# A load moved behind masks, a cast moved to GpSimd and weight sums moved up in a fused attention and feed-forward kernel

## The chip, the cores and the metric

The kernel runs on one core of a Trainium2 chip. The metric is the device time of one execution in microseconds (us). Before the change the median of three runs is 211.47 us (211.43 to 211.76).

The core has TensorE (PE; its weight loads are shown as PEld), VectorE (DVE), ScalarE (ACT) and GpSimd (POOL), which compute, and SyncE (SP), which here only issues transfers. Each works through its own queue in order. A transfer (DMA) is issued by SP, ACT or POOL and then carried out by 16 DMA engines that all queues share.

## What is computed

Linear attention with decay over 4 batches, 8 heads, 768 positions of 64 values, and then a feed-forward layer of width 2048 on the 512 joined head outputs:

```python
    for b in range(nb):
        qb, kb, vb = (q[:, :, sl], k[:, :, sl], v[:, :, sl])
        intra = np.einsum('bhic,bhjc->bhij', qb, kb) * Dmask[None]
        intra = np.einsum('bhij,bhjd->bhid', intra, vb)
        inter = np.einsum('bhid,bhde->bhie', qb * lam_pow[None], kv_state)
        out[:, :, sl] = intra + inter
        kb_dec = kb * rev_pow[None]
        kv_state = lam_block[None, :, None, None] * kv_state + np.einsum('bhsd,bhse->bhde', kb_dec, vb)
...
    xn = (x - mu) / np.sqrt(var + 1e-06) * g_ln
    ch = np.maximum(xn @ w_ch1, 0.0) @ w_ch2
    return (x + ch).astype(np.float32)
```

## The kernel before

**Units.** The work is cut into 12 units. A unit is 256 positions of one batch with all 8 heads, two tiles of 128 rows. Units 0 to 3 are the first 256 positions of the four batches (no state comes in), 4 to 7 the next, 8 to 11 the last. In the change's name, pairs of tiles are counted from one: the second pair is unit 1, the fourth is unit 3.

**What a unit goes through.**
1. Its k, q and v (512 KB each in float32) are loaded into a pool with three buffers for each of the three (`load_in`, `load_window`, `fill`). SP issues them at line 76, from unit 6 on in two halves at line 80.
2. k is cast to bfloat16 (`in_k_one`, line 231; `in_k`, line 215), q is multiplied with the decays (`in_q_one`, line 236; `in_q`, line 226), v likewise (`in_v`, line 242, into `vb`).
3. k and q are transposed: units 0 to 2 by TensorE (`transpose_pe`, line 250), the later ones by a DMA transpose that SP issues (`transpose_dma`, line 257), into `kqT`.
4. TensorE makes the scores of two halves (`scores`, line 273, into two PSUM buffers `sc`), VectorE masks them into bfloat16 (`mask`, line 283). Unit 0's second half is masked in two steps: ScalarE copies it (line 290), VectorE multiplies (line 294).
5. TensorE makes the new states (`kv`, line 307). In unit 3 VectorE decays the first of them (line 313), adds the second (`state_sum`, line 317), and GpSimd decays that one (line 313).
6. `av` (line 419) and `inter` (line 432) sum the output in PSUM. `inter` is called twice; between the calls VectorE makes a small copy of the output, `seen` (`reader`, line 443), for which the second call waits.
7. The rows are copied and centred (`norm`, lines 458 to 470), transposed (`to_xT`, lines 486 and 493) and go into the feed-forward part.

**Feed-forward.** `mlp(g)` gives two kinds of steps for unit g: `m1`, a product with part of W1 (line 530, at the start line 641) with a relu by ScalarE (line 533 or 644), and `m2`, a product with W2. For units 0 to 3, `m2` is plain (line 667); VectorE evicts a finished tile (line 691). From unit 4 on it is a scheme with seven products for eight (line 565) that needs sums of blocks of W2, called `wt`. VectorE makes these once, in `w_sums(c, n)` for four chunks c of W2: n = 0 is two subtractions or additions (lines 787 and 788), n = 1 two more (790 and 791), each 128x512 float16 with both inputs in SBUF. Their first use is in unit 4's part, at 100 us.

**Weights.** W1 and W2 come in four chunks each, cast on the way by GpSimd's transfer queue (`load_w1`, line 117; `load_w2`, line 120). `load_w1(0)` is issued between the steps of unit 0, chunks 1 to 3 between GpSimd's work for unit 1, in this order: q, first half; chunk 1; q, second half; chunk 2; v of unit 1; chunk 3. GpSimd then waits for chunk 2 to land (`behind`, line 728) before it clears one column of unit 2's k buffer (`open_in` with a gate, line 91). SP's load of that k waits for this column, so that it can't start earlier. Unit 3's load is held back by a gate of the same kind.

**The order** is written out by hand: a long list of calls at the end of the kernel, in which `units(n)` takes the next n steps of the feed-forward list `plan`. Each call puts its instructions at the end of the queues of the engines that it names. The PSUM tag `mm` has four buffers that go round among m1, m2, `kv` and others.

At the start, `load_window(1)` issues k, q and v of unit 1 on SP directly behind those of unit 0. Around unit 3, the order is: states of unit 2 (`s0(2)`), the casts of unit 3's k on VectorE and the rest of its inputs on GpSimd, its two transposes, v of unit 4, two steps, `s3(2)` with the first `inter` and the copy `seen`, two steps, `s4(2)` with the second `inter`. After it, the steps number 8 to 12 stand around the transposes of unit 2's rows; then GpSimd's inputs of unit 4 and this:

```python
    units(5)
    w_sums(0, 0)
    w_sums(0, 1)
    units(2)
    w_sums(1, 0)
    units(1)
    s1(3)
```

The five steps are the four of unit 1's second tile in `m2`, whose last one is evicted by VectorE, and the first `m1` step of unit 2; the three others are `m1` steps of unit 2.

Of the kernel before, what the change touches and what calls it, by code (L numbers as in the profile page):

```python
# [17 lines left out]
def kernel(  # L18
# [11 lines left out]
    nc = tc.nc  # L30
# [35 lines left out]
    qkv_in = {}  # L66
# [5 lines left out]
    def fill(got, name, u, hs, eng=None):  # L72
        eng = eng or nc.sync
        src = dict(k=k, q=q, v=v)[name]
        if u < LB:
            eng.dma_start(got[:, hs], source(src, u, hs))  # L76
            return
        cc, b = divmod(u, B)
        for j in range(2):
            eng.dma_start(got[:, hs, j * D:(j + 1) * D],  # L80
                          src[b, hs, cc * W + j * C:cc * W + (j + 1) * C, :].rearrange("h p d -> p h d"))
# [6 lines left out]
    def open_in(u, gate):  # L88
        qkv_in[u] = {name: inp.tile([128, H, 2 * D], F32, tag=name + "in", name=name + "in") for name in "kqv"}
        if gate:  # L90
            nc.gpsimd.memset(qkv_in[u]["k"][:, 0, 0:1], 0.0)

    def load_in(u, name, eng):
        got = qkv_in[u][name]
        fill(got, name, u, slice(0, H), eng)
        qkv_in[u][name] = got.rearrange("p h (j d) -> p h j d", j=2)

    def load_window(u, after_pool=False, parts=1):
        got = {name: inp.tile([128, H, 2 * D], F32, tag=name + "in", name=name + "in") for name in "kqv"}
        if after_pool:  # L100

            nc.gpsimd.memset(got["k"][:, 0, 0:1], 0.0)
        n = H // parts
        order = [(name, i) for i in range(parts) for name in "kq"] + [("v", i) for i in range(parts)]
        for name, i in order:
            hs = slice(i * n, (i + 1) * n)
            fill(got[name], name, u, hs)
        qkv_in[u] = {name: f.rearrange("p h (j d) -> p h j d", j=2) for name, f in got.items()}
# [89 lines left out]
    def open_window(u):  # L198
        kq = wk.tile([128, 2, NP, 2, 2, D], BF16, tag="kq", bufs=3, name="kq")
        vb = wk.tile([128, H, 2, D], BF16, tag="vb", bufs=4, name="vb")  # L200
        st[u] = dict(kq=kq, vb=vb)
        if u < XB:
            st[u]["kqT"] = wk.tile([128, 2, NP, 2, 128], BF16, tag="kqT", bufs=3, name="kqT")

    def part(a, dst, hs):

        return dst[:, a, hs.start // 2:hs.stop // 2].rearrange("p a j e d -> p a e j d")
# [3 lines left out]
    def in_k(u, eng, hs=ALL):  # L211
        src = qkv_in[u]["k"][:, hs].rearrange("p (a e) j d -> p a e j d", e=2)
        dst = part(0, st[u]["kq"], hs)
        for j in range(2):
            (eng.copy if eng is nc.scalar else eng.tensor_copy)(dst[:, :, :, j], src[:, :, :, j])
# [13 lines left out]
    def in_k_one(u, eng, j):  # L229
        src = qkv_in[u]["k"].rearrange("p (a e) j d -> p a e j d", e=2)  # L230
        (eng.copy if eng is nc.scalar else eng.tensor_copy)(part(0, st[u]["kq"], ALL)[:, :, :, j], src[:, :, :, j])

    def in_q_one(u, eng, j):
        src = qkv_in[u]["q"].rearrange("p (a e) j d -> p a e j d", e=2)
        lq = (lam_q[:, :, j] if u < LB else lam_p[:, 0, :]).rearrange("p (a e) -> p a e", e=2)
        eng.tensor_tensor(part(1, st[u]["kq"], ALL)[:, :, :, j], src[:, :, :, j],  # L236
                          lq[:, :, :, None].to_broadcast([128, NP, 2, D]), op=ALU.mult)

    def in_v(u, eng, hs=ALL):
        n = hs.stop - hs.start  # L240
        lv = lam_v[:, hs, :, None] if u < LB else lam_p[:, 1, hs, None, None]
        eng.tensor_tensor(st[u]["vb"][:, hs], qkv_in[u]["v"][:, hs], lv.to_broadcast([128, n, 2, D]), op=ALU.mult)  # L242
# [17 lines left out]
    def scores(u, hf, early=False):  # L260

        s = st[u]
        kT, qT = s["kqT"][:, 0], s["kqT"][:, 1]
        if early:
            sc = [mm_tile([128, 2, 2, 128], F32, f"sce{e}") for e in range(2)]
        else:
            sc = [ps.tile([128, 2, 2, 128], F32, tag="sc", bufs=2, name=f"sc{e}") for e in range(2)]
        mA = wk.tile([128, 2, 2, 2, 128], BF16, tag=f"mA{hf}", name=f"mA{hf}")
        for i in range(2):
            for jk in range(2):  # L270
                for ab in range(2):
                    for e in range(2):
                        nc.tensor.matmul(sc[e][half[ab], i, jk, :], lhsT=kT[half[e], 2 * hf + i, jk, half[ab]],  # L273
                                         rhs=qT[half[e], 2 * hf + i, :, half[ab]],
                                         start=(i == 0 and jk == 0), stop=(i == 1 and jk == 1), skip_group_check=True)
        s[f"mA{hf}"] = mA
        s[f"sc{hf}"] = sc
# [8 lines left out]
    def mask_by_act(u, hf):  # L286

        s = st[u]
        for e in range(2):
            nc.scalar.copy(s[f"mA{hf}"][:, e], s[f"sc{hf}"][e])  # L290
        kp = keep_h.rearrange("p a b t -> p a (b t)")
        for e in range(2):
            m = s[f"mA{hf}"][:, e]
            nc.vector.tensor_tensor(m, m, kp[:, None, :, :].to_broadcast([128, 2, 2, 128]), op=ALU.mult)

    def kv(u, tag="mm"):

        s = st[u]
        cc, b = divmod(u, B)
        n_ab = 2 if (cc + 1) * W < S else 1  # L300
        bufs = dict(mm=4, sc=2, po=1)[tag]
        pk = [ps.tile([128, 2, NP, D], F32, tag=f"po{ab}" if tag == "po" else tag, bufs=bufs, name=f"pk{ab}")[:, 0] for ab in range(n_ab)]
        for p in range(NP):
            for j in range(2):
                for e in range(2):
                    for ab in range(n_ab):
                        nc.tensor.matmul(pk[ab][half[e], p, :], lhsT=s["kq"][half[ab], 0, p, j, e],
                                         rhs=s["vb"][half[ab], 2 * p + e, j],
                                         start=(p == 0 and j == 0), stop=(p == NP - 1 and j == 1), skip_group_check=True)
        s["pk"] = pk  # L310
# [9 lines left out]
    def new_state(u, ab, eng):  # L320

        s = st[u]
        b = u % B
        if ab == 1 and len(s["pk"]) == 1:
            return
        old = state.get(b)
        if ab == 0:
            s["S"] = [(old, old)]
        Sn = wk.tile([128, NP, D], BF16, tag="S", bufs=12, name="Sn")
        if old is None and eng is nc.scalar:  # L330
            for p in range(NP):
                nc.scalar.activation(Sn[:, p], s["pk"][ab][:, p], ACT.Identity, scale=lam_s[:, p:p + 1])
        elif old is None:
            decay(nc.vector, Sn, s["pk"][ab])
        else:
            tmp = s.pop("tmp", None) or state_sum(u, ab)
            decay(eng, Sn, tmp)
        state[b] = Sn
        if ab == 0:
            s["S"].append((Sn, Sn))  # L340
# [394 lines left out]
            nc.tensor.matmul(t, lhsT=ident, rhs=rhs, start=True, stop=True)  # L735

    open_window(0)
    load_window(1)
    in_k(0, nc.vector, HA)
    transpose_pe(0, 0, (0, 1))  # L740
    keep_busy(1, "po0")
# [22 lines left out]
    mask(0, 0)  # L764
    scores(0, 1, early=True)
    mask_by_act(0, 1)
    kv(0)
    new_state(0, 0, nc.scalar)
    av(0, (0, 1))
# [11 lines left out]
    def w_sums(c, n):  # L781
        v = w2[c].rearrange("p (k e) d -> p k e d", e=2)
        w = DM // 2
        b11, b12, b21, b22 = v[:, :, 0, 0:w], v[:, :, 0, w:], v[:, :, 1, 0:w], v[:, :, 1, w:]
        t1, t2, t3, t4 = (wt[c][:, :, i] for i in range(4))
        if n == 0:
            nc.vector.tensor_tensor(t1, b12, b11, op=ALU.subtract)  # L787
            nc.vector.tensor_tensor(t3, b12, b22, op=ALU.add)
        else:
            nc.vector.tensor_tensor(t2, b11, t3, op=ALU.subtract)  # L790
            nc.vector.tensor_tensor(t4, t2, b21, op=ALU.add)
# [28 lines left out]
    def s1(u):  # L820
        kv(u)
        scores(u, 0)
        new_state(u, 0, nc.gpsimd)
        mask(u, 0, (0,))
        new_state(u, 1, nc.gpsimd)
        mask(u, 0, (1,))
# [195 lines left out]
    def units(n):  # L1022
        for _ in range(n):
            f, *a = next(steps)
            f(*a)
# [15 lines left out]
    units(2)  # L1041
    s0(2)
    open_window(3)
    in_k_one(3, nc.vector, 0)
    in_k_one(3, nc.vector, 1)
    in_q_one(3, nc.gpsimd, 0)
    in_q_one(3, nc.gpsimd, 1)
    in_v(3, nc.gpsimd)
# [21 lines left out]
    in_q_one(4, nc.gpsimd, 0)  # L1070
    in_q_one(4, nc.gpsimd, 1)
    in_v(4, nc.gpsimd)
    units(5)
    w_sums(0, 0)
    w_sums(0, 1)
    units(2)
    w_sums(1, 0)
    units(1)
    s1(3)
    store(0)  # L1080
    transpose_dma(4, 0)
# [273 lines left out]
```

## Time and profile before

| what | value |
|---|---|
| median of three runs | 211.47 us |
| the profiled execution | 212.06 us |
| its span | 210.4 us |
| mean granted TensorE clock | 0.997 |
| moved over the span | 36.39 MB, 173 GB/s |
| PE busy from 15 to 20 us | 3.55 of 5.00 us |
| PE busy from 45 to 50 us | 3.96 of 5.00 us |
| PE busy from 60 to 65 us | 4.45 of 5.00 us |
| PE busy from 80 to 100 us | 20.00 of 20.00 us |

The span is the time from the first to the last thing that the profiler records; the device time has another 1.7 us around it. A line of the timeline gives start, duration, engine, line of the code, operation, what is written and read, how many instructions are taken together, and in brackets the idle time before it with what ended it. A line of the waits gives the engine and line that waited, for whom, the total in us, how often, and the longest. The chain in order of time follows back from the last instruction what released each step; SPq is SP's queue of transfers. In the view of the DMAs q1 is SP's queue and q0 is GpSimd's, each with packets, megabytes and the share of the 16 engines.

### The profile page before, as it was taken

What the parts mean: (1) busy time and instruction counts of PE and PEld (TensorE: products, weight loads), DVE (VectorE), ACT (ScalarE), POOL (GpSimd) and SP (SyncE); (2) the same over time, 40 slices, a digit from 0 to 9 for tenths busy, and PEclk for the clock granted to TensorE, in tenths of its full rate; (3) what the DMA queues carried; (4) which work ended last, traced back from release to release, by engine and by line L of the source; (5) the groups of instructions that cost most, each with busy time, mean ns of one, the idle gap of its engine ahead of it and who ended that gap; (6) DMA issues with size and microseconds to landing.
All of it is one profiled execution on the core that took longest, in us unless ns stands there. A gap on an engine that the chain in (4) does not pass through costs nothing.

```text
span 210.4 us, 7229 instructions
## 1 busy us (share of the span) xinstructions
PE 197.7 (94%) x3099; PEld 157.1 (75%) x3099; DVE 132.8 (63%) x274; ACT 121.6 (58%) x280; POOL 83.8 (40%) x116
## 2 busy tenths in 40 slices
PE   2987999989989999999999999999999999999991
PEld 0476889535666577568888898888888888888881
DVE  2683660534585966659698785667877857865252
ACT  3864679617155368528656675585596575652620
POOL 4657049218469150527246350862274202002020
PEclk9999999999999999999999999999999999999998
DMA  4999999999999998995896999897989020078403
GB/s 113 300 253 190 185 272 198 194 287 247 219 301 222 218 182 151 191 247 93 174 230 101 184 200 155 195 219 114 214 155 199 7 50 3 21 143 280 113 12 89
DMA packets 91042, 36.39 MB, mean 173 GB/s; under 512 B 65153, under 2 KB 88193, under 8 KB 91010
## 3 DMA queue, kind: packets, MB, share of 16 engines
q1 hardware_dynamic: 86400, 31.53, 72.8%
q0 software_dynamic: 4224, 4.19, 12.7%
q8 instruction: 24, 0.39, 0.8%
q10 hardware_dynamic: 386, 0.20, 0.4%
q14 instruction: 8, 0.07, 0.1%
HBM read 27.27 MB, written 6.29 MB: 160 GB/s over the span
## 4 chain that ended last, share of the span: by engine, by line
PE 69%; DMA 15%; DVE 5%; POOL 4%; SPq 3%; issue 1%; POOLq 0%; ACT 0%; DVEq 0%
PE pm L530 31%; PE pm L667 11%; DMA qin<-in_q_dram 7%; PE pwd L565 6%; PE pwa L565 6%; PE pwc L565 6%; DMA kin<-in_k_dram 5%; DMA w<-in_moe_w_ch_dram 3%; PE pwb L565 3%; SPq L76 3%; PE po L432 1%; DVE wt L787 1%; POOL kq L226 1%; DVE x L578 1%; PE po L406 1%
## 5 line engine op out<-in xcount | busy, mean ns | idle before, releaser
L530 PE MATMUL pm<-xT,w 128*128 128x256 bf16 x736 | 84.7, 273 | 0.0
L530 PEld LDWEIGHTS <-w 128*128 128x128 bf16 x736 | 70.5, 98 | 9.5 <-DVE Smid L388 0.3
L533 ACT ACTIVATE hT<-pm 128x512 f16<-128x512 f32 x92 | 53.9, 599 | 30.1 <-PE pm L530 30.0
L667 PE MATMUL pm<-w,hT 128*128 128x512 f16 x128 | 30.2, 380 | 0.0
L565 PEld LDWEIGHTS <-hs 128*128 128x128 f16 x256 | 24.9, 98 | 2.9
L590 POOL TENSOR_TENSOR x<-ev_u,x 128x256 f32<-128x256 f32 x8 | 5.9, 738 | 49.7 <-ACT ev_u L589 38.3
L313 POOL TENSOR_TENSOR Sn<-Stmp,lam_s 128x256 bf16<-128x256 f32 x16 | 9.8, 616 | 38.0 <-DVE Stmp L317 19.8
L548 DVE TENSOR_TENSOR hs<-hT 128x1024 f16<-128x1024 f16 x16 | 12.8, 800 | 15.6 <-ACT hT L533 15.6
L283 DVE TENSOR_TENSOR mA<-sc,keep 128x512 bf16<-128x512 f32 x20 | 13.1, 684 | 13.4 <-PE sc L273 13.4
L667 PEld LDWEIGHTS <-hT 128*128 128x128 f16 x128 | 11.7, 98 | 12.1
L565 PEld LDWEIGHTS <-hT 128*128 128x128 f16 x192 | 18.8, 98 | 2.2
L458 ACT ACTIVATE x<-po 128x512 f32<-128x512 f32 x18 | 10.6, 590 | 9.2 <-PE po L432 5.7
L460 DVE SCALAR_TENSOR_TENSOR xc<-po,nmean,g_row 128x512 bf16<-128x512 f32 x18 | 12.9, 745 | 3.6 <-ACT nmean L459 3.5
L242 POOL TENSOR_TENSOR vb<-vin,lam_v 128x1024 bf16<-128x1024 f32 (+1 forms) x7 | 11.8, 1691 | 4.2 <-DMA vin<-in_v_dram 4.2
L503 ACT ACTIVATE sq<-x,nmean 128x512 bf16<-128x512 f32 x18 | 12.9, 719 | 0.3
L242 POOL TENSOR_TENSOR vb<-vin,lam_p 128x1024 bf16<-128x1024 f32 x6 | 11.4, 1896 | 2.9 <-DMA vin<-in_v_dram 2.9
L236 POOL TENSOR_TENSOR kq<-qin,lam_q 128x512 bf16<-128x512 f32 x8 | 8.2, 1046 | 5.4 <-DMA qin<-in_q_dram 5.4
L494 ACT COPY xT<-xt 128x512 bf16<-128x512 bf16 x10 | 5.8, 585 | 7.7 <-PE xt L493 7.7
L236 POOL TENSOR_TENSOR kq<-qin,lam_p 128x512 bf16<-128x512 f32 x9 | 9.3, 1042 | 2.5 <-DMA qin<-in_q_dram 2.5
L578 DVE SCALAR_TENSOR_TENSOR x<-pwd,rstd,x 128x256 f32<-128x256 f32 x16 | 7.7, 482 | 3.5 <-POOL x L598 3.5
L578 DVE SCALAR_TENSOR_TENSOR x<-pwa,rstd,x 128x512 f32<-128x512 f32 (+1 forms) x16 | 9.1, 613 | 0.8
L565 PE MATMUL pwa<-w,hT 128*128 128x256 f16 x64 | 9.6, 273 | 0.0
(129 smaller groups left out, 301.1 us busy)
## 6 DMA issues: line engine op xcount, KB each, us to landing
out_dram<-x SPq DMA_DIRECT2D x22, 256.0 KB, 3.8
w<-in_moe_w_ch_dram POOLq DMA_DIRECT2D x8, 512.0 KB, 7.8
kin<-in_k_dram SPq DMA_DIRECT2D x14, 256.0 KB, 4.9
qin<-in_q_dram SPq DMA_DIRECT2D x14, 256.0 KB, 5.0
vin<-in_v_dram SPq DMA_DIRECT2D x14, 256.0 KB, 5.2
kin<-in_k_dram SPq DMA_DIRECT2D x5, 512.0 KB, 6.2
qin<-in_q_dram SPq DMA_DIRECT2D x5, 512.0 KB, 7.0
vin<-in_v_dram SPq DMA_DIRECT2D x5, 512.0 KB, 7.6
```

Source lines behind the costliest of these rows:

```text
L236: eng.tensor_tensor(part(1, st[u]["kq"], ALL)[:, :, :, j], src[:, :, :, j], lq[:, :, :, None].to_broadcast([128, NP, 2, D]), op=ALU.mult)
L242: eng.tensor_tensor(st[u]["vb"][:, hs], qkv_in[u]["v"][:, hs], lv.to_broadcast([128, n, 2, D]), op=ALU.mult)
L283: nc.vector.tensor_tensor(s[f"mA{hf}"][:, e], s[f"sc{hf}"][e], kp[:, None, :, :].to_broadcast([128, 2, 2, 128]), op=ALU.mult)
L458: nc.scalar.activation(x, po, ACT.Copy, accum_out=sm)
L460: nc.vector.scalar_tensor_tensor(xc, in0=po, scalar=nm, in1=g_row, op0=ALU.add, op1=ALU.mult)
L503: nc.scalar.activation(sq, s["x"][:, ab], ACT.Square, bias=s["nmean"][:, ab:ab + 1], accum_out=ss[:, ab:ab + 1])
L530: nc.tensor.matmul(pm[:, b, :], lhsT=w1[n // W2K][:, kk, (n % W2K) * 128:(n % W2K + 1) * 128], rhs=xT_of[g][:, kk, 0:N], start=(b == 0 and ...
L533: nc.scalar.activation(hT[:, u * NB:(u + 1) * NB, 0:N], pm, ACT.Relu)
L548: nc.vector.tensor_tensor(s13, b[:, :, 1:2, :].to_broadcast([128, n, 2, 128]), b[:, :, 0:4:3, :], op=ALU.subtract)
L565: nc.tensor.matmul(pr[bank], lhsT=lhs(r), rhs=rhs, start=(first and r == 0), stop=(r == KB // 2 - 1), skip_group_check=True)
L578: nc.vector.scalar_tensor_tensor(out, in0=in0, scalar=r[ab], in1=in1, op0=ALU.mult, op1=ALU.add)
L667: nc.tensor.matmul(acc[i], lhsT=hT[:, kk, i * 128:(i + 1) * 128], rhs=w2[kk // W2K][:, kk % W2K, :], start=(kk == 0), stop=(kk == KB - 1))
```

## The change

Three parts.

1. `load_window(1)` becomes `open_in(1, False)` with loads of k and q only. The load of v stands behind `mask_by_act(0, 1)`: VectorE clears one column of v's buffer after the two masking products of line 294, and SP's load of v waits for this.
2. The two casts of unit 3's k move from VectorE's queue to GpSimd's, in front of the q products of that unit.
3. The three `w_sums` calls move two steps up. In VectorE's queue, the four sums of chunk 0 now stand in front of the eviction of unit 1's second tile instead of behind it; the two of chunk 1 stand directly behind that eviction. On the other engines no order changes by this.

```diff
     open_window(0)
-    load_window(1)
+    open_in(1, False)
+    load_in(1, "k", nc.sync)
+    load_in(1, "q", nc.sync)
     in_k(0, nc.vector, HA)
...
     mask_by_act(0, 1)
+    nc.vector.memset(qkv_in[1]["v"][:, 0, 0:1], 0.0)
+    load_in(1, "v", nc.sync)
     kv(0)
...
     open_window(3)
-    in_k_one(3, nc.vector, 0)
-    in_k_one(3, nc.vector, 1)
+    in_k_one(3, nc.gpsimd, 0)
+    in_k_one(3, nc.gpsimd, 1)
     in_q_one(3, nc.gpsimd, 0)
...
-    units(5)
+    units(3)
     w_sums(0, 0)
     w_sums(0, 1)
     units(2)
     w_sums(1, 0)
-    units(1)
+    units(3)
     s1(3)
```

## The prediction, before the changed kernel was run

> **What bounds the kernel now.** I read the page's busy shares and slices first, then the waits of PE, then the chain in order of time, then the timeline around each PE gap. TensorE is busy 94% of the span, and from 80 us on it is never idle for more than 0.1 us in a stretch of 20: what is to be won lies before 65 us.
>
> ```profile
> PE 197.7 (94%) x3099; PEld 157.1 (75%) x3099; DVE 132.8 (63%) x274; ACT 121.6 (58%) x280; POOL 83.8 (40%) x116
> ...
> PE   2987999989989999999999999999999999999991
> ...
> DMA  4999999999999998995896999897989020078403
> ```
>
> The slices show PE falling to 7 or 8 only in the first 65 us, and the DMA engines full up to 80 us. The waits of PE over the whole span name the gaps:
>
> ```profile
> PE pm1t L641 <- DMA w<-in_moe_w_ch_dram: 1.5, 1, 1.5
> PE po L432 <- DVE seen L443: 1.0, 1, 1.0
> PE sc L273 <- DVE mA L283: 0.6, 1, 0.6
> ```
>
> Each is one wait: 1.45 us until W1's first chunk has landed (PE could go at 16.07, goes at 17.53), 1.04 us and 0.55 us until VectorE has done something. The chain in order of time shows who sets the second:
>
> ```profile
> 34.95 11.44 DMA kin<-in_k_dram
> 46.39 0.02 issue
> 46.41 0.76 DVE kq L231 x2
> 47.17 0.09 DVE seen L443
> 47.26 0.04 issue
> 47.30 0.31 PE po L432 x8
> ```
>
> k of unit 3 takes 11.44 us to land; its casts stand in VectorE's queue ahead of the small copy `seen` for which PE waits. The timeline of VectorE from 55 to 65 us shows the third:
>
> ```profile
> 57.88 0.43 DVE L791 TENSOR_TENSOR wt<-wt,w 128x512 f16<-128x512 f16 x1
> 58.23 2.12 DVE L787 TENSOR_TENSOR wt<-w 128x512 f16<-128x512 f16 x1
> 60.28 0.41 DVE L788 TENSOR_TENSOR wt<-w 128x512 f16<-128x512 f16 x1
> 60.61 0.41 DVE L313 TENSOR_TENSOR Sn<-pk,lam_s 128x256 bf16<-128x256 f32 x1
> 60.95 0.68 DVE L283 TENSOR_TENSOR mA<-sc,keep 128x512 bf16<-128x512 f32 x1
> ```
>
> One sum over W2 takes 2.12 us where its neighbours take 0.42, and unit 3's state and masks stand behind it. PE's third gap (62.05 to 62.60) is the wait for the second mask, which ends at 62.55.
>
> **What the Trainium skill says.** "SBUF — State Buffer", section "Who interferes with whom": a VectorE tensor_tensor with two inputs in SBUF and a GpSimd instruction that reads SBUF exclude each other for a whole instruction, and the one that issues second blocks; an instruction with one SBUF input is free of this. The trace agrees: GpSimd's vb of unit 4 runs from 57.92 for 2.15 us and the sum issued at 58.23 ends at 60.35; the masks (one input in PSUM) keep 0.68 us beside GpSimd's work at 63 us. "DMA: Bandwidth & Descriptors", section "Queues, rings and completion order": each DMA engine takes turns between the queues that have work. Here this holds in part: from 14 to 16 us both queues move, but k of unit 3, issued at 34.95, has no packet on SP's queue before 38 us while GpSimd's queue takes 115.8% (the view of the DMAs from 35 to 38 us). Same page, section "Latency and other measured facts": a first byte on SP's path after about 0.6 us. The trace has more: k of unit 2 is issued at 23.88, its first packets come at 25.0, so I use 1.2 us.
>
> **Part 1: v of unit 1.** SP issued it at 7.90, behind k and q of unit 1. Now SP waits for a one-column memset that stands on VectorE behind the two products of line 294, which end at 12.27; the memset costs about 0.06 (line 164 has one) in front of `stats`, which waits for PE until 12.90: nothing. Nothing stands behind SP's wait but k of unit 2, which is issued at 23.88 anyway. So v is issued at 12.4, 4.5 us later, though its packets move much less: k and q fill SP's queue until 13.2 (q lands at 13.23), and v's packets come after that.
>
> W1's first chunk (issued 8.09) has its first packets at 11.4 and lands at 17.5. From 13 to 16.5 v's packets are beside it, about 0.44 MB of v's 0.52. How much is taken from between them cannot be read off:
> - Lower end: v starts after the usual 1.2 us, at 13.6. Then only the 0.04 MB that SP's queue moved between 13 and 14 us are displaced, worth 0.2 us at the 0.2 MB per us that GpSimd's queue makes alone (0.40 MB from 32 to 34 us). I take 0 as the end.
> - Upper end: v is not served until the chunk is through, as k of unit 3 was not. The chunk has moved 0.2 MB by 13.0; the other 0.32 take 1.6 us, and PE finds it there when it is ready: 1.45. What comes next caps this: chunk 3 of W1 lands at 26.3 (20.41 and 5.9) and is used at 27.55, so 1.2 us earlier is all that PE can use.
>
> I take the middle, 0.6. The cover on v's own side: v lands at 18.56 now, GpSimd's vb ends at 20.45, PE wants it for kv(1) at 22.22, or 21.6 with 0.6 gained: 1.1 us of room. Behind vb on GpSimd stands the issue of W1's chunk 3, with 0.6 us left. A v that comes 0.6 us late is free.
>
> **Part 2: k of unit 3 cast by GpSimd.** VectorE loses two casts (0.76 us) and, above all, the 3.54 us of waiting for the landing. `seen` then runs right after its matmuls (44.43), and PE goes on at 46.26 instead of 47.30: 1.04 us. What is late next? The W2 chunks: the third lands at 42.3 for its use at 45.3, the fourth at 46.0 for 49.5, 3 us or more; less 1.64 there is still 1.4. GpSimd gains two casts at 0.585 (rows of line 231 at 51.95: 1.17 for two). It stood idle until q of unit 3 landed at 48.04 (4.53 us of waiting); k lands at 46.39, so the casts end at 47.6: cost nothing. The first DMA transpose of unit 3 is issued at 47.86, behind q of unit 4 on SP (until 47.76): no change. If q came together with k, GpSimd's row would slide by 1.17; the transposes land at 55.2 and 56.0, and PE wants them at 59.6 less 1.64: hidden too.
>
> **Part 3: sums two units earlier.** The number of instructions is the same. The four sums of chunk 0 now stand ahead of the last eviction of unit 1 (line 691, 55.97) and behind the third one, which ends at 53.68, less 1.64: 52.0. There GpSimd is busy without a break until 55.13 (vb of 3, casts and q of 4). Six sums at 0.42 are 2.5 us; GpSimd has 3.2 left (two casts 1.17, two q products 2.05). If they take turns, all is over at 57.7. The eviction waits until about 56 and needs 0.75; the PSUM buffer it frees is wanted by the fourth m1 unit at 58.5 less 1.64, 56.9: just free. GpSimd's q products end near 56.9 instead of 55.13, and then it waits for v of unit 4 (57.92) as before. So the sums end 0.2 us before the long vb starts, unit 3's kv ends on PE at 59.81 less 1.64, and VectorE takes Sn, mask, Stmp, mask in 1.94 us (60.61 to 62.55) from there, 2.0 after kv's end; PE comes back for the second mask's buffer 2.2 us after that end (59.81 to 62.05). The stall goes: 0.5, with 0 where the sums block each other, and a price below for the collision.
>
> **Sum.** 0.6 + 1.04 + 0.5 = 2.1 us. The profiled execution took 212.06, 1.7 of it around the span of 210.4; the median of the runs is 211.47. Span 208.3, profiled execution 209.9, median 209.4. Later stages should carry it through: transposes of unit 4 land by 67.8 and are wanted at 71.7, vb of 5 is there 17 us early, and behind 80 us loads and transposes are issued by the progress of compute itself.
>
> **Rivals.**
> - v gets going at once and W1's chunk is no earlier. For it: only 0.04 MB lie between the two starts. Against: k of unit 3, kept waiting by the same kind of traffic. Parts 2 and 3 alone: 1.5, 209.9.
> - The collision returns. If the last sum is still to issue when v of unit 4 lands at 57.92, it is blocked until 60.0 again, the mask ends at 62.5, and PE, however early it came, goes on at 62.6 as before: everything won until then is lost there. 211.4, no change. For it: 0.2 us of room. Against: taking turns may cost GpSimd rather than VectorE.
> - Slower: v starved. If SP's queue is not served while chunks 0 to 2 of W1 follow one another (as with k and v of unit 3: 11.4 and 13.7 us), v lands with chunk 2 at 23.6 instead of 18.56. vb then ends at 25.5, kv(1) loses 3.3 us on PE, chunk 3 is issued at 25.5 and lands at 31.4 against a use that has become 30.9: 3.8 lost. Less 1.5 from the other parts: 2.3 slower, 213.8. It decides from a landing at about 21.8 on. Against: chunk 1 is issued at 14.43 and its packets come near 17, so between 15 and 17 us the engines are free for 0.5 MB.
>
> **How the numbers follow.** Forecast 0.47, v without effect 0.20, collision 0.13, starved 0.13, mixtures that end between 0.07. A measurement of this kernel tells 0.2% (0.4 us) from no change. Faster: 0.47 and 0.20 and part of the mixtures, 0.72; same 0.13; slower 0.15. Predicted 209.4; its own range, with part 1 between 0 and 1.2 and part 3 between 0 and 0.6, is 208.6 to 210.5. The range for 8 in 10 takes in the collision and leaves the starved case out: 208.5 to 211.5.
>
> **What would show it.** Part 1: chunk 0's wait of PE at 16 to 17.5 shorter than 1.45, vb of unit 1 starting no later than 19.2. Part 2: no wait of PE for `seen` near 46, two casts on GpSimd ending before q of unit 3 is used. Part 3: no sum of 2.1 us in front of unit 3's masks; the four sums of chunk 0 stretched beside GpSimd's work near 52 to 56. I am wrong if PE waits for vb of unit 1 or for W1's chunk 3, or if PE goes on with unit 3's second scores at 62.6 after all.

## The result, and the profile after

| | before | after |
|---|---|---|
| median of 20 runs | 211.44 us (210.52 to 214.56) | 211.00 us (210.00 to 212.91) |
| ratio, 95% interval | | 0.9989 (0.9968 to 1.001) |
| the profiled execution | 212.06 us | 210.06 us |
| its span | 210.4 us | 208.3 us |

The forecast was 2.1 us less than before, 209.4 us. The runs show 0.44 us between the medians, and the interval of the ratio includes no change. The two profiled executions, though, stand 2.0 us apart, nearly what was forecast. So the two traces alone would have seemed to confirm a sum that the runs do not. Some executions, one of before's 20 here, are 1.5% or more above the fastest of their kernel; the ratios leave them out, and so do the medians and means of the experiments.

What the trace of after shows, read in the order of the prediction. First the waits of PE over the whole span (engine and line that waited, for whom, total us, how often, longest):

```profile
PE g_all L180 <- DMA g_one<-in_moe_g_ln_dram: 4.0, 1, 4.0
PE po L419 <- issue: 0.7, 1, 0.7
PE pm L530 <- DMA w<-in_moe_w_ch_dram: 0.4, 2, 0.3
PE po L419 <- DVE mA L283: 0.3, 1, 0.3
```

All three waits that the prediction went after are gone: for W1's first chunk (1.45), for `seen` (1.04) and for the second mask of unit 3 (0.55). Two kinds are new, a halt of 0.7 us at line 419 that waits for nothing the profile shows ("issue"), and two waits for later chunks of W1. Both lie in the timeline of PE from 15 to 29 us:

```profile
15.89 1.91 PE L641 MATMUL pm1t<-xT,w 128*128 128x128 bf16 x16
...
21.15 1.92 PE L530 MATMUL pm<-xT,w 128*128 128x256 bf16 x16 [0.26 <-DMA w<-in_moe_w_ch_dram]
23.00 0.61 PE L419 MATMUL po<-vb,mA 64*64 64x64 bf16 x52
24.30 0.29 PE L419 MATMUL po<-vb,mA 64*64 64x64 bf16 x12 [0.70 <-issue]
...
27.33 1.05 PE L530 MATMUL pm<-xT,w 128*128 128x256 bf16 x8 [0.16 <-DMA w<-in_moe_w_ch_dram]
```

PE starts unit 0's feed-forward at 15.89 instead of 17.53, 1.64 us earlier. At unit 1's second product with its states the lead is down to 0.55 (25.65 against 26.20), and at the first half-step of `m1` behind the transposes to 0.22 (27.33 against 27.55). A wait of PE for W1's chunk 3, here 0.16 us, is one of the signs that the prediction named for being wrong.

The timeline of VectorE around unit 3's load and the W2 sums:

```profile
43.90 0.17 DVE L443 COPY seen<-po 128x8 f32<-128x8 f32 x1 [1.60 <-PE po L432]
...
51.93 1.20 DVE L791 TENSOR_TENSOR wt<-w 128x512 f16<-128x512 f16 x1
53.05 0.83 DVE L792 TENSOR_TENSOR wt<-w 128x512 f16<-128x512 f16 x1
53.91 0.71 DVE L794 TENSOR_TENSOR wt<-w,wt 128x512 f16<-128x512 f16 x1
54.66 1.15 DVE L795 TENSOR_TENSOR wt<-wt,w 128x512 f16<-128x512 f16 x1
55.74 0.74 DVE L691 SCALAR_TENSOR_TENSOR x<-pm,rstd,x 128x512 f32<-128x512 f32 x1
```

(The lines of the helper stand four further down in this kernel: 787 is 791.) `seen` waits for PE alone and no longer stands behind a cast. The four sums take 3.9 us beside GpSimd's work instead of 1.7, as expected, and the eviction behind them still ends in time.

The same places on GpSimd: k of unit 3 lands at 47.27, its casts end before q of unit 3 is used at 48.93, and vb of unit 4 starts when all six sums are over. The v that it needs lands 1.3 us later than before (59.20 against 57.92):

```profile
47.27 1.17 POOL L231 CAST kq<-kin 128x512 bf16<-128x512 f32 x2 [4.27 <-DMA kin<-in_k_dram]
48.93 2.06 POOL L236 TENSOR_TENSOR kq<-qin,lam_q 128x512 bf16<-128x512 f32 x2 [0.49 <-DMA qin<-in_q_dram]
...
59.20 1.91 POOL L242 TENSOR_TENSOR vb<-vin,lam_v 128x1024 bf16<-128x1024 f32 x1 [2.47 <-DMA vin<-in_v_dram]
```

So all three waits are gone in this execution. The question for the experiments is which part of the 2.1 us exists outside this one pair of executions.

### The profile page after: what moved, and what is told of

The parts are those of the page before. It is cut to its first block, busy times and chain, and to the rows that moved or that the text cites. A ratio compares the mean times of both kernels' runs of the same rounds, so it can differ in the third digit from the quotient of the medians.

```text
span 208.3 us, 7233 instructions
## 1 busy us (share of the span) xinstructions
PE 196.9 (95%) x3099; PEld 156.6 (75%) x3099; DVE 133.7 (64%) x273; ACT 121.7 (58%) x280; POOL 86.2 (41%) x118
## 4 chain that ended last, share of the span: by engine, by line
PE 59%; DMA 21%; POOL 8%; SPq 4%; DVE 3%; ACT 1%; issue 1%; POOLq 0%; ACTq 0%; DVEq 0%
PE pm L530 29%; DMA qin<-in_q_dram 13%; PE pwd L565 6%; PE pwc L565 6%; PE pwa L565 6%; DMA w<-in_moe_w_ch_dram 4%; PE pm L667 3%; POOL kq L236 3%; PE pwb L565 3%; SPq L76 3%; DMA vin<-in_v_dram 2%; DMA kin<-in_k_dram 2%; POOL vb L242 2%; SPq L257 1%; POOL kq L226 1%
## 5 line engine op out<-in xcount | busy, mean ns | idle before, releaser
L667 PE MATMUL pm<-w,hT 128*128 128x512 f16 x128 | 30.2, 380 | 0.0
L548 DVE TENSOR_TENSOR hs<-hT 128x1024 f16<-128x1024 f16 x16 | 14.7, 921 | 16.2 <-ACT hT L533 16.2
L236 POOL TENSOR_TENSOR kq<-qin,lam_p 128x512 bf16<-128x512 f32 x9 | 9.8, 1103 | 1.5 <-DMA qin<-in_q_dram 1.5
L565 PE MATMUL pwb<-w,hT 128*128 128x256 f16 x64 | 9.2, 273 | 0.0
```

Of the source, the lines that this page charges most:

```text
L548: nc.vector.tensor_tensor(s13, b[:, :, 1:2, :].to_broadcast([128, n, 2, 128]), b[:, :, 0:4:3, :], op=ALU.subtract)
L565: nc.tensor.matmul(pr[bank], lhsT=lhs(r), rhs=rhs, start=(first and r == 0), stop=(r == KB // 2 - 1), skip_group_check=True)
L667: nc.tensor.matmul(acc[i], lhsT=hT[:, kk, i * 128:(i + 1) * 128], rhs=w2[kk // W2K][:, kk % W2K, :], start=(kk == 0), stop=(kk == KB - 1))
```

## The experiments

Kernels in one group share the runs of before beside them. A ratio is against those runs, as recorded with its 95% interval; 0.001 is 0.21 us. It need not be the quotient of the two medians, nor that of the means of all these runs, which is 0.9970 for e2, 0.9984 for e3 and 0.9982 for e14. So a difference of 0.2% between two rows is within the spread.

| kernel | parts | median, us | before beside it | ratio, 95% interval | span of its trace |
|---|---|---|---|---|---|
| e1 | 1 | 211.80 | 211.52 | 1.0011 (0.9988 to 1.0034) | 210.6 |
| e2 | 2 | 211.01 | 211.52 | 0.9961 (0.9941 to 0.9981) | 208.7 |
| e3 | 3 | 211.32 | 211.52 | 1.0003 (0.9983 to 1.0022) | 212.7 |
| e4 | 2, 3 | 211.12 | 211.52 | 0.9963 (0.9941 to 0.9985) | 209.0 |
| e5 | 1, 2, 3 | 210.71 | 211.53 | 0.9969 (0.9948 to 0.9989) | 209.3 |
| e6 | 1, 2 | 210.89 | 211.53 | 0.9968 (0.9948 to 0.9988) | 208.3 |
| e7 | 1, 2, 3, W1's chunk 1 earlier | 212.59 | 211.53 | 1.0051 (1.0024 to 1.0078) | 210.3 |
| e8 | 2, W1's chunk 1 earlier | 213.51 | 211.53 | 1.0081 (1.0048 to 1.0114) | 211.2 |
| e12 | 1, 2, 3, W1's chunk 3 earlier | 210.94 | 211.35 | 0.9978 (0.9955 to 1.0002) | 210.0 |
| e13 | 2 in another form | 210.52 | 211.34 | 0.9959 (0.9941 to 0.9977) | 208.3 |
| e14 | 3, again | 210.94 | 211.34 | 0.9985 (0.9963 to 1.0008) | 209.5 |

Of three more only one execution each is used, for its trace: before twice (e9, e10) and after with more instructions on PE (e11).

### Each part alone, and two together: e1 to e4

The edits are the hunks of the diff, one at a time.

e1, the load of v of unit 1 alone:

```diff
-    load_window(1)
+    open_in(1, False)
+    load_in(1, "k", nc.sync)
+    load_in(1, "q", nc.sync)
...
     mask_by_act(0, 1)
+    nc.vector.memset(qkv_in[1]["v"][:, 0, 0:1], 0.0)
+    load_in(1, "v", nc.sync)
```

> Part 1 alone (v of unit 1 behind the masks). Theory A (part 1 gives its gain back before 25 us, in other executions more than that): PE starts W1's first chunk about 1.5 us earlier, waits again for v's product, for W1's chunk 1 or chunk 2 by 25 us, and the time is 0 to 1 us above before (ratio 1.000 to 1.005), the 1.0 us wait for `seen` near 46 us still there. Theory B (part 1 is good for 0.6 us as forecast): 0.6 us below before, ratio 0.997.

e2, the casts alone:

```diff
-    in_k_one(3, nc.vector, 0)
-    in_k_one(3, nc.vector, 1)
+    in_k_one(3, nc.gpsimd, 0)
+    in_k_one(3, nc.gpsimd, 1)
```

> Part 2 alone (k of unit 3 cast by GpSimd). Theory A (parts 2 and 3 pay in every execution): no wait for `seen` near 46 us, 1.0 us below before, ratio 0.995. Theory C (before, the landing of that k varies from execution to execution, and the profiled one was a late one): the typical gain is 0 to 0.4 us, ratio 0.998 to 1.000, although the trace has no wait for `seen`.

e3, the sums alone (`units(5)` to `units(3)`, and `units(1)` behind them to `units(3)`):

> Part 3 alone (sums two units earlier). Theory A: the 2.1 us sum in front of unit 3's masks is gone, 0.5 us below before, ratio 0.9975. Theory C (where the long product of GpSimd falls varies): 0 to 0.2 us, ratio 0.999 to 1.000.

e4 has the edits of e2 and e3:

> Parts 2 and 3 without part 1. Theory A (the two gains add, and part 1 costs about 1 us in a typical execution): 1.5 us below before, ratio 0.993, and below the changed kernel. Theory C: as the changed kernel, 0.4 us below before, ratio 0.998.

The profiled execution of e3 took 214.44 us, so its trace is not used. Part 2 alone wins 0.8 us by its ratio, 0.6 by the means of all runs, and part 3 adds nothing to it (0.9963 against 0.9961). Part 1 alone wins nothing. The waits of PE in e1 show its bill: chunk 0's wait is gone as in after, and one of 1.9 us for chunk 3 has come, with the halt at line 419.

```profile
PE pm L530 <- DMA w<-in_moe_w_ch_dram: 1.9, 1, 1.9
PE po L432 <- DVE seen L443: 1.2, 1, 1.2
PE po L419 <- issue: 0.5, 1, 0.5
```

Why part 3 adds nothing is in e2. With part 2 alone, the sums stand where they stood before the change, behind the eviction. These are the last sum and what follows on VectorE, and vb of unit 4 on GpSimd, in the timelines of e2:

```profile
58.41 0.42 DVE L788 TENSOR_TENSOR wt<-w 128x512 f16<-128x512 f16 x1
58.89 0.42 DVE L313 TENSOR_TENSOR Sn<-pk,lam_s 128x256 bf16<-128x256 f32 x1
59.23 0.68 DVE L283 TENSOR_TENSOR mA<-sc,keep 128x512 bf16<-128x512 f32 x1
...
59.84 1.90 POOL L242 TENSOR_TENSOR vb<-vin,lam_v 128x1024 bf16<-128x1024 f32 x1 [3.22 <-DMA vin<-in_v_dram]
```

vb starts 1.0 us after the last sum has ended. No sum takes 2.1 us, and PE doesn't wait for the second mask. Part 2 had already taken the third gap away. It did so less by bringing the sums forward than by what happened to the load. The last sum is issued at 58.41, which is after the 57.92 at which vb started before; what lets it through is that v of unit 4 lands 1.9 us later. SP issues this load behind unit 3's two transposes (line 257). In the timelines of SP this is before, then e2:

```profile
52.70 0.58 SPq L76 DMA_DIRECT2D vin<-in_v_dram  x1
...
54.73 0.57 SPq L76 DMA_DIRECT2D vin<-in_v_dram  x1
```

e6 and e13, whose sums also stand in the old place, are alike: last sum at 57.96 and 58.16, vb at 59.15 and 59.35.

### The whole change again, and parts 1 and 2: e5 and e6

> The changed kernel once more, on the chip of the three below. Theory D (part 1 lets PE start W1's first chunk 1.5 us earlier, and PE then waits for W1's last chunk, whose landing is as late or later): a wait of 0.3 to 2 us for W1 between 25 and 29 us in the trace, time as part 2 alone, ratio 0.996 to 0.998. Theory E (the changed kernel's first 20 runs were unlucky): ratio 0.993.

> Parts 1 and 2 without part 3. Theory D, with part 3 worth nothing once part 2 has moved VectorE forward: the same as the changed kernel within 0.2%, and no sum of 2 us in front of unit 3's masks. Theory A (part 3 is worth its 0.5 us by itself): 0.5 us slower than the changed kernel.

e5 puts the change clear of no change, at 0.9969, where the first measurement had 0.9989; the intervals overlap, and the two stand for 0.2 to 0.65 us. Neither e5 nor e6 is faster than part 2 alone. Part 1 on top of part 2, with or without part 3, is not seen to be worth anything: e6 against e2 is +0.0007, e5 against e4 is +0.0006, and e1 against before +0.0011. In e5's trace the bill is larger than in after's:

```profile
PE pm L530 <- DMA w<-in_moe_w_ch_dram: 1.2, 2, 0.7
PE po L419 <- issue: 0.9, 1, 0.9
```

That is 0.69 for chunk 1, 0.94 for the halt and 0.51 for chunk 3, 2.1 us together, more than chunk 0 brought.

### Can the lead of part 1 be kept? e7, e8 and e12

If part 1 wins 1.64 us at chunk 0 and loses it to the next chunks, an earlier chunk 1 or 3 should keep it. e7 is after, e8 is part 2 alone, each with this:

```diff
-    in_q(1, nc.gpsimd, HA)
     load_w1(1)
+    in_q(1, nc.gpsimd, HA)
```

> The changed kernel with W1's chunk 1 issued in GpSimd's idle time, in front of unit 1's q product instead of behind its first half (3 us earlier). Theory D: chunks 1 to 3 come one after another without the pause near 16 us, chunk 3 lands 1 us earlier or more, PE's wait for it goes, and 0.5 to 1.2 us are won against the changed kernel. If W1's last chunk is not what eats part 1, nothing changes.

> Part 2 alone with the same early chunk 1. Theory D: nothing is won against part 2 alone, since without part 1 PE is held by chunk 0 until 17.5 us and does not wait for the later chunks: ratio 0.996 as part 2 alone. If an earlier chunk 1 helps by itself, it is faster than part 2 alone by as much as the kernel above is faster than the changed one.

Both became slower than before, by 0.5 and 0.8%. GpSimd's timeline of e8 says why (a line L117 is the issue of a W1 chunk):

```profile
10.92 0.81 POOL L117 DMA_DIRECT2D w<-in_moe_w_ch_dram  x1
...
15.50 0.81 POOL L117 DMA_DIRECT2D w<-in_moe_w_ch_dram  x1
22.16 1.89 POOL L242 TENSOR_TENSOR vb<-vin,lam_v 128x1024 bf16<-128x1024 f32 x1 [5.85 <-DMA vin<-in_v_dram]
```

With chunk 1 issued at 10.92 instead of 14.43, while chunk 0 is still on its way, v of unit 1 lands at 22.16 instead of 18.56, although e8 issues it on SP where before does. In e7, where it is issued behind the masks, it lands at 21.08. This is the prediction's slower rival, v starved, at work: what sets it off is the place of chunk 1, not the place of v. PE waits 1.6 us for vb in e8 and 2.5 in e7.

e12 is after with chunk 3 issued ahead of v's product:

```diff
     load_w1(2)
-    in_v(1, nc.gpsimd)
     load_w1(3)
+    in_v(1, nc.gpsimd)
```

> The changed kernel with W1's chunk 3 issued in front of unit 1's v product on GpSimd (at about 17.3 instead of 20.1 us, in idle time). Theory D1 (chunk 3 lands late because it is issued late): it lands by 26.5, PE's wait for it goes, 0.3 to 1 us faster than the changed kernel, ratio below 0.995. Theory D2 (GpSimd's queue is full from 17 to 25 us and the end of chunk 3 is held by k and q of unit 2 on the same engines): no gain, 0.995 to 0.999.

Chunk 3 no longer holds PE up, but in e12's trace chunk 1 does, for 1.24 us at 22.72. At 0.9978 (0.9955 to 1.0002) it is not better than e5. In this trace moving one chunk has only moved the wait to another.

### The halt at line 419: e11

PE halts inside one run of 64 matmuls whose operands are all there. In the traces of after, e1, e5 and e12 this comes after exactly 52 of the 64, for 0.53 to 0.94 us, and before never halts there, nor does e6, where chunk 0 is later and PE gets there at 23.86. In the DMA view of after from 22 to 23 us a third queue shows up beside GpSimd's q0:

```profile
q0 software_dynamic: 181, 0.17, 112.3%
q8 instruction: 1, 0.02, 6.0%
```

The packet of q8 starts at 22.12 in after and takes 0.96 us; PE goes on at 24.30. The Trainium skill, "Runtime: NRT & Kernel Launch", section "Instruction fetch mechanics", says that an engine's instructions come in blocks of 16 KiB over a DMA queue of its own, which fits one packet of 0.02 MB. It calls the cost of going from one block to the next mostly hidden; if this halt is such a step, that is not so here. If PE has run out of fetched instructions, the halt belongs to a place in the program and must move by as many instructions as are put in front. e11 puts 8 matmuls with their 8 weight loads ahead of unit 1's transposes; they write a scratch buffer that nothing reads:

```diff
     load_w2(1)
+    t8 = ps.tile([128, 512], F32, tag="sc", bufs=2, name="idle8")
+    for _ in range(8):
+        nc.tensor.matmul(t8[:, 0:64], lhsT=ident, rhs=ident[:, 0:64], start=True, stop=True)
     transpose_pe(1, 0, (0, 1), nc.vector)
```

> The changed kernel with eight more weight loads and eight more matmuls of 64 columns in PE's queue near 13 us (they compute nothing that is used). In the three traces with part 1 that show it, PE halts in unit 1's av for 0.5 to 0.9 us after 52 of 64 matmuls, without a named cause, 1.3 us after a 16 KB packet of the instruction queue. Theory F (PE has run out of fetched instructions, since part 1 brought it forward and the fetch is not earlier): the halt comes eight matmuls earlier, after 44 of 64. If the halt is a wait for data of av, it stays after 52.

PE's timeline of e11:

```profile
22.79 0.54 PE L419 MATMUL po<-vb,mA 64*64 64x64 bf16 x44
24.46 0.35 PE L419 MATMUL po<-vb,mA 64*64 64x64 bf16 x20 [1.13 <-issue]
```

The halt has moved from 52 to 44: by 8 matmuls and 8 weight loads, the 16 instructions that were added. A wait for data would have stayed at its matmul. In all five traces that have this halt, e11 among them, exactly 351 matmuls stand in front of it. There is a second halt of this kind, near 95 us, in e4, e6 and e11, each time behind 1502 matmuls. In the timelines of PE it comes after 19 of 48 matmuls in e4 and e6 and after 11 in e11, again 8 earlier. Here is what is left behind it in e4, then in e11:

```profile
95.75 3.34 PE L530 MATMUL pm<-xT,w 128*128 128x256 bf16 x29 [0.27 <-issue]
...
95.86 4.21 PE L530 MATMUL pm<-xT,w 128*128 128x256 bf16 x37 [0.67 <-issue]
```

The first halt follows the second packet of q8, the second halt the eleventh, 1.2 to 1.5 us after the packet's end each time. Between the two places the traces have 2304 records of PE's instructions, 256 for each of the nine packets. So the halts stand at the ends of blocks of instructions, and PE has run out of those that were fetched. No run changes the fetch itself.

In before the packet comes at 22.40, much the same time, but PE reaches this place at 24.45 and finds the block there. Part 1 lets PE arrive 1.4 us earlier and doesn't bring the block forward. Part 1 is not the only way to such a halt: e4, which has one at 95 us, is without part 1.

### Is the collision a matter of one execution? e9 and e10

The 2.12 us sum was seen in one execution of before, so two more executions of before were profiled.

> The kernel before, looked at once more. Theory C (the two later waits are different in each execution): the wait for `seen` near 46 us is other than 1.04 us (0 to 3), and the 2.1 us sum in front of unit 3's masks is not there. If both gaps belong to the kernel, they come back at 1.0 and 0.5 us.

> The same kernel, a third execution of it: as in the run before this one. Theory C gives a third pair of values; otherwise 1.0 and 0.5 us again.

It recurs in both. VectorE's timeline of e9:

```profile
58.90 2.12 DVE L787 TENSOR_TENSOR wt<-w 128x512 f16<-128x512 f16 x1
...
61.28 0.41 DVE L313 TENSOR_TENSOR Sn<-pk,lam_s 128x256 bf16<-128x256 f32 x1
```

vb of unit 4 starts at 58.66 in e9, so this sum came 0.24 us too late; in e10 it is 57.97 and 58.21. PE waits 0.5 to 0.6 us in each. It isn't certain, however: in e1, whose sums are no earlier, v of unit 4 lands so late (59.88) that they get through. The collision is a race between the sums and a landing. The wait for `seen` varies far more: 1.04 in before, 1.1 in e9, 0.4 in e10, 1.2 in e1.

### What of part 2 counts, and part 3 once more: e13 and e14

Two points were open: whether part 2 acts by taking the wait off VectorE's queue or by giving the work to GpSimd, and whether part 3 alone has any effect. In e13 the casts stay on VectorE and move behind the norms of unit 2:

```diff
     open_window(3)
-    in_k_one(3, nc.vector, 0)
-    in_k_one(3, nc.vector, 1)
     in_q_one(3, nc.gpsimd, 0)
...
-    transpose_dma(3, 0)
-    transpose_dma(3, 1)
-    load_in(4, "v", nc.sync)
...
     s4(2)
+    in_k_one(3, nc.vector, 0)
+    in_k_one(3, nc.vector, 1)
+    transpose_dma(3, 0)
+    transpose_dma(3, 1)
+    load_in(4, "v", nc.sync)
```

> Before, with one edit: the two casts of unit 3's k stay on VectorE, but are emitted behind the second inter of unit 2 and its norms, with the two transposes and v of unit 4 behind them. Theory B (part 2's whole effect is that VectorE's queue is no longer blocked by the landing of k in front of the copy seen): no wait of PE for seen near 46 us, and the time of part 2 alone, ratio 0.996 (210.7 to 211.1 us). Rival (part 2 gains because VectorE is relieved of the casts, or because GpSimd does them): at most half of that, 0.998 or above. Both theories: casts end near 48.5, the transposes of unit 3 are issued about where they were, at 48 to 49 us, and are wanted 9 us later.

> Part 3 alone once more, with five rounds on the chip of the run beside it. As the prediction had it (0.5 us on its own): ratio 0.9975, no wait of PE for the second mask of unit 3 near 62 us. Theory C' (its place gains nothing by itself, since without part 2 the sums are still late): ratio 0.999 to 1.001. In either case the wait for seen near 46 us stays, 0.4 to 1.2 us.

e13 wins what part 2 wins, 0.9959. VectorE's timeline:

```profile
44.23 0.17 DVE L443 COPY seen<-po 128x8 f32<-128x8 f32 x1 [1.60 <-PE po L432]
45.08 0.75 DVE L460 SCALAR_TENSOR_TENSOR xc<-po,nmean,g_row 128x512 bf16<-128x512 f32 x1 [0.68 <-ACT nmean L459]
...
47.93 0.75 DVE L231 CAST kq<-kin 128x512 bf16<-128x512 f32 x2
```

The casts are still VectorE's work, 0.75 us of it, but no longer stand in front of `seen`, which runs 3.7 us before them and waits for PE alone. It is the queue behind the wait that cost, not the work of the casts. e13 does not single out `seen`, however: in it v of unit 4 lands late as well, so that the third gap is gone too.

e14 puts part 3 alone at 0.9985 with an interval from 0.9963 to 1.0008, e3 at 1.0003. Neither ratio separates part 3 from nothing. By the means of all runs the two are 0.35 and 0.38 us below before, each with about 0.4 of noise, so a gain of a few tenths isn't excluded either. In e14's trace the sums do escape: the last ends at 58.08, vb starts at 58.39, and PE has no wait for the second mask.

## Why the prediction was wrong

The span falls into three stretches at two landmarks in PE's timelines: the start of the 32 matmuls of line 641 near 30 us, and unit 3's first `inter` (line 432) near 64 us.

| trace | parts | to 641 | 641 to unit 3's inter | from there to the end |
|---|---|---|---|---|
| before | | 29.88 | 35.45 | 145.0 |
| e9 | | 30.51 | 35.49 | 144.9 |
| e10 | | 30.20 | 34.78 | 145.0 |
| e1 | 1 | 30.63 | 34.88 | 145.1 |
| e14 | 3 | 30.72 | 33.84 | 144.9 |
| e2 | 2 | 30.01 | 33.61 | 145.1 |
| e13 | 2, other form | 29.64 | 33.61 | 145.0 |
| e4 | 2, 3 | 30.16 | 33.61 | 145.3 |
| e6 | 1, 2 | 29.45 | 33.60 | 145.3 |
| e5 | 1, 2, 3 | 30.32 | 33.77 | 145.2 |
| after | 1, 2, 3 | 29.31 | 33.61 | 145.4 |

**Part 1: "I take the middle, 0.6".** This step failed. Its upper end came true where it was worked out: in after SP's queue moves nothing from 13 to 14 us, chunk 0 lands at 15.7 instead of 17.5, and PE lost its wait (in e6 the chunk lands at 16.9, and 0.85 us of the wait stays). v itself comes no later, at 18.27 against 18.56. What failed is the cap, "1.2 us earlier is all that PE can use", from chunk 3's landing at 26.3 in before. Three things stood closer. Chunk 3 itself lands later, at 27.3 in after and 28.6 in e1, though it is issued 0.3 us earlier and v has landed by then. Chunk 1, which the cap didn't look at, holds PE for 0.26 us in after and 0.69 in e5. And the fetch of PE's instructions, which the prediction didn't know of, takes 0.5 to 0.9. The first column shows the result: with part 1 29.31 to 30.63, mean 29.9, without it 29.64 to 30.72, mean 30.2. In the runs the term is zero within their intervals, and e1's leaves 0.6 out. Why the later chunks land later wasn't tried apart.

**Part 2: 1.04.** The mechanism was right: in every trace with part 2 `seen` waits for PE alone, and e13 shows that it is enough to take the casts from in front of it. The size was read from one execution. The five traces that have the casts in their old place (before, e9, e10, e1, e14; e3's left out) give 1.04, 1.1, 0.4, 1.2 and 0.2, mean 0.8. The runs of part 2 give 0.6 to 0.9 (e2, e13). That this is about the same doesn't confirm the term, because in the traces part 2 removes the third gap as well. The covers held: the transposes and q of unit 3 were never late for PE. But "the first DMA transpose of unit 3 is issued at 47.86 [...] no change" did not hold. In e2 it is issued at 48.98 and v of unit 4 behind it 2.0 us later than before, which decides the race of part 3.

**Part 3: 0.5.** This step failed by counting twice: it prices a gap that in e2, e6 and e13 doesn't outlive part 2. The prediction takes 1.64 us off the times of the sums in their new place, compares them with vb of unit 4 at its old 57.92, and never asks what becomes of the sums in the old place. By the same working they would be free there too: the blocked sum is issued at 58.23 less 1.64, 56.6, and the last one 0.33 later; with part 2's 1.04 alone it is 57.2 and 57.5. The runs come to the same end by another way. e2 has its last sum only at 58.41, because the first one takes 1.24 us beside GpSimd's q product, and it passes because vb starts at 59.84. Why SP comes to the load later wasn't tried apart, and it isn't certain: in e4 v of unit 4 is issued at 52.70 and vb starts at 57.93, and there the sums of the new place end at 57.36. So the relief comes without part 3 in e2, e6 and e13, and part 3 may be what gives it in e4.

The second column says the same: 34.8 to 35.5 without parts 2 and 3, 33.8 with part 3 alone, 33.6 with part 2, and 33.6 to 33.8 with both. Either part takes the third gap; they don't add. The 33.8 owes something to luck, since the wait for `seen`, which part 3 doesn't touch, was only 0.2 in e14. The stretching of the sums beside GpSimd came out as expected. The eviction behind them cost nothing in after, e4, e5 and e14; in e7, e11 and e12 PE waited 0.2 to 0.5 us for it.

**The sum.** Of the 2.1, the runs leave 0.6 to 0.9, from part 2; for the whole change they show 0.2 to 0.65. The pair of profiled executions shows 2.0 on the span by another sum: 0.57 from the first column, 1.84 from the second, and 0.4 given back in the third. That this equals the forecast is luck: the execution of before was long for its kernel (212.06 against a median of 211.44) and the one of after short (210.06 against 211.00), which makes 1.6 of the 2.0. One thing stays open: in the second column part 2 saves 1.5 us on the mean of the four traces without parts 2 and 3, about twice what its runs show. The trace of one execution doesn't tell what the others looked like.

**The rivals.** "v without effect" (209.9) was nearest in part 1's size, though by another way: it had an effect that was given back. The collision with vb didn't return with part 2. In e8, though, two sums stretched to 1.2 and 1.3 us beside GpSimd's q products, and PE waited 0.44 us for the second mask. The starved v is real, as e7 and e8 show, but it needs chunk 1 earlier.

## What to carry to other kernels

When two edits remove stalls on one path, rework the timeline after the first before pricing the second: a stall that is a race may be gone with the first edit alone, here because the landing moved as well. When a wait for a transfer is removed, everything else that PE would need earlier has to be listed, the later transfers with their landings under the new traffic and the instructions themselves. And a stall in front of a landing should be sized from several executions; here it ran from 0.2 to 1.2 us.

## What was not expected of the hardware

PE can run dry of instructions in straight-line code. The halts came while transfers kept the DMA engines at 102 to 126%, took 0.3 to 1.1 us, ended 1.2 to 1.5 us after the end of a packet of the instruction queue (23.09 to 24.30 in after, 24.36 to 25.83 in e12), and moved by 16 instructions when 16 were put ahead of them.

A transfer on SP's queue can be kept waiting by the mere spacing of GpSimd's transfers. With W1's chunks issued at 7.96, 10.92 and 15.50, a 512 KB load landed at 22.16; with 8.09, 14.43 and 16.39 it landed at 18.56.
